# Retention attention and a sine-gated feed-forward: a re-planned table of steps, without dummy transfers and with last stores of 128 rows

## The chip, the cores and the metric

The kernel runs on one core of a Trainium2 chip. The metric is the device time of one execution in microseconds; the times of a kernel are the median of several executions, and one more execution is recorded by the profiler. The engines are PE (matrix products, with its weight loads shown as PEld), DVE, ACT and POOL (element-wise work), and SP, which here only issues transfers (DMAs).

## The reference

Two parts follow each other. The first is a causal attention without softmax for 8 batches, 8 heads, 576 positions and 64 numbers per head; its scores are damped by the distance. Its result is read as 4608 tokens of 512 numbers and goes through a feed-forward with a sine.

```python
scores = scale * np.matmul(q, k.transpose(0, 1, 3, 2))
rel = pos[:, None] - pos[None, :]
Dmat = np.where(rel >= 0, gamma[:, None, None] ** rel[None, :, :], 0.0)
x = np.matmul(scores * Dmat, v)          # read as (4608, 512)
h = x @ w_in                             # 512 x 2048
s = np.sin(alpha * h)
g = h + s * s / (alpha + 1e-09)
out = g @ w_out                          # 2048 x 512
```

## The kernel before

**Blocks.** The first 512 tokens of each batch form blocks 0 to 7. The last 64 tokens of all batches together form block 8, the "ends". A block goes through attention (of its batch), the product with w_in in 16 chunks of 128 columns (`project`, four matmuls of 128 x 512 each), `sine` and `square` (mostly ACT), `product` (DVE), and the product with w_out. Blocks 0 to 2 do this last product plainly (`gemm2`, stored by `finish`); blocks 3 to 8 save one of eight quarter products by the scheme of Strassen and Winograd: `weight_sum` and `row_sum` prepare sums, `part_product 8 3` is the third of the seven products of block 8 (16 matmuls of 128 x 256 for each half), and `after_product` adds its bank to a kept part on DVE and stores the result.

**The table.** The whole order is a table of some 1200 lines, written out by hand, one step a line; a loop runs them, and each engine executes its instructions in the order in which the steps stand. Nothing reorders them. A step such as `crossed 5 0 q @qT2` names the batch 5, the half 0 of its tokens, the operand, and after the @ the buffer that its result gets. Six buffers raw0 to raw5 take all loads of 256 tokens in turn, so a load waits until the cast that reads its buffer has ended. Tags such as m0, h2 or op name banks of PSUM, where PE's products are kept until another engine has read them.

**From a load to PE.** `load 5 q 1` has SP fetch the second 256 tokens of batch 5's queries as 512 KB (L1358); keys and values of batches 4 to 7 come in four transfers of 128 KB (L1353). `cast` (L1404, L1330 for values) scales and rounds them to 16 bits, mostly on POOL. `crossed` (L1426) has SP issue a transposing transfer, which gives PE keys and queries with the head dimension on the partitions (tiles kT and qT). Batches 0 and 1 are transposed on PE (`turn`, `take`). Loads with the last number 2 fetch the last 64 tokens of a batch (L1365; tiles qs, ks, vs). `at.outer` multiplies keys and values on PE (L1514), `at.scores` queries and keys (L1572).

**SP's queue.** SP issues loads, transposes and stores one after the other; when one has to wait (for a cast, for a buffer, for the result to store), all behind it wait as well. Eight semaphores serve SP's transfers in turn, so that each also waits for the landing of the one eight issues earlier. `fill_up` (L1930) issues a dummy transfer of 16 KB that takes a place in this turn.

**The last stores.** Block 8 holds 64 tokens of each of eight batches. A tile `osb` of 128 rows holds two batches, whose rows lie 576 rows apart in the output; `store` writes each half of 64 rows with its own transfer (L1868).

Of the kernel before, what the change touches and what calls it, by code (L numbers as in the profile page):

```python
# [32 lines left out]
invert_alpha
cast 0 v 0 A @v162
# [4 lines left out]
take 0 q 0 A @qT1  # L39
# [16 lines left out]
cast 0 v 1 A @v163
load 1 q 1 @raw5
# [3 lines left out]
keep_busy 1 h1  # L61
# [25 lines left out]
take 1 q 0 V @qT0  # L87
# [16 lines left out]
sine 0 6 @s3  # L104
project 0 7 m1
sine 0 7 @s0
project 0 0 op
square 0 7 A @ss0
sine 0 0 @s2
# [3 lines left out]
load 1 k 0 @raw2  # L113
load_w_out 0
load_w_out 1
cast 1 k 0 G @k163
project 0 4 m0
sine 0 4 @s0
square 0 4 A @ss0
# [4 lines left out]
sine 0 8 @s2  # L124
square 0 8 A @ss2
# [6 lines left out]
take 1 k 0 V @kT1  # L132
sine 0 11 @s1
at.more 0 3 @s320
square 0 11 G @ss1
product 0 11
sine 0 9 @s2
square 0 9 G @ss0
product 0 9
sine 0 5 @s0  # L140
square 0 5 A @ss2
project 0 10 m0
sine 0 10 @s3
# [6 lines left out]
sine 0 14 @s0  # L150
square 0 14 A @ss0
project 0 12 h1
sine 0 12 @s0
# [4 lines left out]
sine 0 13 @s2  # L158
# [4 lines left out]
sine 0 15 @s2  # L163
load 1 v 0 @raw3
cast 1 v 0 G @v162
# [11 lines left out]
cast 1 k 1 G @k162  # L177
# [7 lines left out]
cast 1 v 1 A @v163  # L185
product 0 15
turn 1 k 1 h0
take 1 k 1 V (1) @kT1
# [13 lines left out]
load 2 q 1 @raw0  # L202
load 2 k 1 @raw1
cast 2 k 1 G @k160
# [3 lines left out]
load 2 k 0 @raw3  # L208
load 3 k 1 @raw4
cast 3 k 1 G @k162  # L210
load 2 v 0 @raw5
load 3 k 0 @raw1
wait_for_w_out 1
load 2 v 1 @raw0
# [4 lines left out]
at.keep 1 0 V @xT0  # L219
at.next_sum 1 3  # L220
crossed 2 1 k @kT0
# [3 lines left out]
crossed 2 1 q @qT1  # L225
crossed 2 0 k @kT3
crossed 2 0 q @qT2
# [14 lines left out]
project 1 6 h1  # L242
gemm2 0 3 h0
sine 1 7 @s3
sine 1 6 @s0
# [4 lines left out]
sine 1 13 @s0  # L250
project 1 8 op
sine 1 8 @s1
square 1 13 V @ss0
product 1 13
square 1 8 V @ss2
square 1 7 V @ss0
product 1 8
project 1 11 h1
sine 1 11 @s2
square 1 11 A @ss3  # L260
# [3 lines left out]
square 1 10 A @ss1  # L264
# [4 lines left out]
sine 1 5 @s1  # L269
square 1 5 A @ss3  # L270
project 1 9 h2
sine 1 9 @s0
# [7 lines left out]
cast 3 k 0 G @k163  # L280
at.more 2 1 @s321
at.more 2 2 @s321
# [7 lines left out]
square 1 9 V @ss3  # L290
product 1 9
at.masked 2 1 1 @ret0
square 1 14 A @ss1
product 1 14
sine 1 1 @s1
square 1 1 A @ss0
# [8 lines left out]
square 1 0 A @ss3  # L305
sine 1 4 @s2
square 1 4 A @ss0
sine 1 3 @s0
square 1 3 A @ss2
# [17 lines left out]
sine 1 15 @s3  # L327
# [5 lines left out]
sine 1 12 @s2  # L333
square 1 12 V @ss2
# [13 lines left out]
crossed 3 1 k @kT1  # L348
cast 4 q 1 G @q160
cast 3 q 1 G @q161  # L350
at.more 3 2 @s320
# [4 lines left out]
crossed 3 0 k @kT0  # L356
# [45 lines left out]
sine 2 0 @s3  # L402
square 2 0 A @ss1
# [28 lines left out]
square 2 13 G @ss3  # L432
# [7 lines left out]
at.more 4 1 @s321  # L440
# [26 lines left out]
sine 2 12 @s1  # L467
# [66 lines left out]
product 3 5
sine 3 4 @s3
at.masked 4 0 0 @ret0
at.scores 4 0 1 m0
cast 5 k 0 G @k162
square 3 4 A @ss2
product 3 4  # L540
at.scores 4 1 0 m1
at.masked 4 1 0 @ret1
finish 2 1
cast 5 v 1 G @v163
cast 5 q 1 G @q160
project 3 8 h2
project 3 10 h1
at.masked 4 0 1 @ret2
sine 3 6 @s2
gemm2 2 8 op  # L550
project 3 9 m0
sine 3 8 @s0
square 3 8 A @ss1
product 3 8
load 5 q 0 @raw4
sine 3 10 @s3
project 3 11 h2
square 3 10 A @ss0
gemm2 2 9 op
gemm2 2 10 op  # L560
crossed 5 0 k @kT1
load 6 v 0 @raw0
gemm2 2 11 op
square 3 6 A @ss2
product 3 6
cast 5 q 0 G @q162
sine 3 9 @s0
square 3 9 A @ss2
product 3 9
sine 3 11 @s2  # L570
square 3 11 A @ss3
finish 2 2
load 1 k 2
project 3 12 h0
at.scores 4 1 1 m1
product 3 10
at.outer 5 (0,1) op h1
at.evict_bank 5 0 A @kvs0
at.evict_bank 5 1 A
at.values 4 0 False m0 relay=G  # L580
product 3 11
project 3 13 h2
at.masked 4 1 1 @ret3
at.values 4 1 False m1 relay=G
row_sum 3 S3 0 V
load 6 k 0 @raw1
sine 3 13 @s2
weight_sum T2 0 V
at.values 4 0 True
at.add_states 4 0  # L590
at.values 4 1 True
weight_sum T3 1 V
cast 6 k 0 G @k161
row_sum 3 S2 0 V
crossed 5 0 q @qT2
sine 3 12 @s3
square 3 12 A @ss3
cast 6 v 0 G @v160
weight_sum T2 1 V
product 3 12  # L600
at.add_states 4 1
load 6 v 1 @raw4
project 3 15 h1
cast 6 v 1 G @v161
square 3 13 A @ss0
product 3 13
gemm2 2 12 op
at.keep 4 0 A @xT1
at.keep 4 1 A
gemm2 2 13 op  # L610
gemm2 2 14 op
weight_sum T1 1 V
sine 3 15 @s3
square 3 15 A @ss3
product 3 15
row_sum 3 S1 0 V
gemm2 2 15 op
finish 2 3
project 3 14 h0
at.to_state 5 0 @s161  # L620
at.scores 5 0 1 m1
at.masked 5 0 1 @ret2
sine 3 14 @s3
square 3 14 A @ss3
product 3 14
load 7 v 0 @raw4
weight_sum T4 0 V
at.more 5 1 @s320
project 4 0 h2
sine 4 0 @s2  # L630
row_sum 3 S3 1 V
part_product 3 1 op
after_product 3 1
square 4 0 A @ss2
product 4 0
weight_sum T1 0 V
project 4 2 m0
sine 4 2 @s0
square 4 2 A @ss3
product 4 2  # L640
at.more 5 2 @s320
project 4 1 h1
sine 4 1 @s3
square 4 1 A @ss1
at.scores 5 0 0 m1
product 4 1
row_sum 3 S2 1 V
crossed 5 1 q @qT3
load 6 q 0 @raw1
cast 6 q 0 G @q162  # L650
weight_sum T4 1 V
project 4 4 h0
sine 4 4 @s0
square 4 4 A @ss0
row_sum 3 S1 1 V
project 4 3 h2
sine 4 3 @s3
at.to_state 5 1
part_product 3 2 - first=1
project 4 6 m0  # L660
square 4 3 A @ss2
product 4 3
crossed 5 1 k @kT1
project 4 5 h1
after_product 3 2
sine 4 6 @s3
sine 4 5 @s1
square 4 5 A @ss2
square 4 6 A @ss3
at.masked 5 0 0 @ret0  # L670
part_product 3 6 op
load 6 q 1 @raw0
product 4 4
at.scores 5 1 0 m1
product 4 5
after_product 3 6
project 4 7 h0
sine 4 7 @s2
square 4 7 A @ss0
project 4 9 h2  # L680
row_sum 3 S4 0 V
sine 4 9 @s2
project 4 8 h1
at.to_state 5 2
product 4 7
part_product 3 7 - first=6
sine 4 8 @s1
square 4 9 A @ss0
at.masked 5 1 0 @ret1
load 6 k 1 @raw2  # L690
product 4 6
square 4 8 A @ss3
at.more 5 3 @s320
project 4 10 h0
sine 4 10 @s2
at.to_state 5 3
after_product 3 7
at.scores 5 1 1 m1
at.masked 5 1 1 @ret3
at.values 5 0 False m0 relay=G  # L700
part_product 3 5 op
square 4 10 A @ss1
at.values 5 0 True
cast 0 q 2 G
at.add_states 5 0
at.keep 5 0 A @xT0
project 4 11 m1
sine 4 11 @s1
row_sum 3 S4 1 V told_to=G
crossed 6 0 k @kT2  # L710
product 4 8
cast 0 k 2 G
after_product 3 5
part_product 3 3 - first=5
product 4 9
product 4 10
after_product 3 3
project 4 12 h2
square 4 11 A @ss1
sine 4 12 @s3  # L720
project 4 13 h0
sine 4 13 @s2
load 2 v 2
square 4 12 A @ss0
load 3 v 2
product 4 11
cast 6 k 1 G @k163
at.values 5 1 False m1 relay=G
at.outer 6 (0,1) op h1
at.evict_bank 6 0 A @kvs0  # L730
at.evict_bank 6 1 A
square 4 13 A @ss3
crossed 6 0 q @qT2
product 4 12
at.values 5 1 True
at.add_states 5 1
part_product 3 4 m0
project 4 14 h1
row_sum 4 S3 0 V
load 7 q 0 @raw1  # L740
after_product 3 4
at.keep 5 1 A
at.more 6 1 @s320
sine 4 14 @s0
square 4 14 A @ss0
cast 6 q 1 G @q162
row_sum 4 S2 0 V
fill_up
project 5 0 m1
row_sum 4 S3 1 V  # L750
sine 5 0 @s2
square 5 0 A @ss2
load 1 v 2
product 4 14
project 4 15 m0
cast 0 v 2 G
at.to_state 6 0 @s161
product 5 0
crossed 6 1 k @kT3
part_product 4 1 op  # L760
project 5 1 h2
at.scores 6 0 1 m1
project 5 3 h1
product 4 13
sine 4 15 @s2
square 4 15 A @ss0
product 4 15
after_product 4 1
part_product 4 2 - first=1
load 7 k 1 @raw0  # L770
sine 5 1 @s2
square 5 1 A @ss0
sine 5 3 @s2
load 2 q 2
square 5 3 A @ss2
project 5 2 h0
row_sum 4 S1 0 V
crossed 6 1 q @qT3
at.masked 6 0 1 @ret2
load 3 q 2  # L780
after_product 4 2
at.more 6 2 @s321
at.more 6 3 @s321
at.to_state 6 3
cast 7 v 0 G @v162
product 5 1
row_sum 4 S2 1 V
row_sum 4 S4 0 V
load 7 k 0 @raw2
cast 7 k 0 G @k161  # L790
at.to_state 6 1
sine 5 2 @s0
square 5 2 A @ss1
product 5 2
project 5 4 h2
sine 5 4 @s0
square 5 4 A @ss3
part_product 4 6 op
product 5 3
row_sum 4 S4 1 V told_to=G  # L800
project 5 5 h0
after_product 4 6
sine 5 5 @s2
product 5 4
square 5 5 A @ss2
project 5 6 h1
sine 5 6 @s0
# [437 lines left out]
def kernel(  # L1245
# [18 lines left out]
    nc = tc.nc  # L1264
# [641 lines left out]
    at = [Attention(b) for b in range(B)]  # L1906
# [136 lines left out]
```

## Time and profile before

| | |
|---|---|
| median of 3 runs | 306.46 us (306.09 to 306.5) |
| profiled execution | 307.99 us, its span 306.3 us |
| mean granted clock of PE | 0.969 |
| busy: PE, DVE, ACT, POOL | 287.7, 220.2, 220.0, 138.0 us |
| transferred | 50.08 MB, mean 164 GB/s |

The span runs from the first to the last recorded instruction or landing; the profiled execution's own time has 1.7 us around it. In a row of a timeline the first number is the start in us, the second the duration, then come the engine, the line, the operation, output and inputs, the number of like instructions joined in the row, and in brackets the idle time ahead of it with what ended it. SPq and ACTq are the issuing of transfers by those engines; a transfer lands later than its issue ends. "Granted clock" is the share of full speed at which PE ran.

### The profile page before, as it was taken

Reading aid. Unit: us, or ns where it says so; the run is one execution under the profiler, and the core shown is the slowest. Engines: PE = TensorE matmul, PEld = TensorE weight load, DVE = VectorE, ACT = ScalarE, POOL = GpSimd, SP = SyncE. Lnnn points to the kernel's source line nnn. Section 1 sums busy time; section 2 is a strip of 40 time slices with the busy share of each in tenths; the row PEclk is TensorE's granted clock in tenths of the full one; section 3 lists DMA queues with packets and bytes.
Section 4 is the critical chain, followed back from the end, with each engine's and each line's share of the span. In section 5 each row is a group of like instructions: output and inputs, shape, how many; then the busy total and the mean of one; then the engine's idle time right before and its main releaser. Section 6 shows DMA issues by size and latency. Waiting matters only on the chain. (4 is left out here: it accounts for less than half of the span.)

```text
span 306.3 us, 8404 instructions
## 1 busy us (share of the span) xinstructions
PE 287.7 (94%) x3480; PEld 183.5 (60%) x3480; DVE 220.2 (72%) x316; ACT 220.0 (72%) x361; POOL 138.0 (45%) x151
## 2 busy tenths in 40 slices
PE   5789999999989999995999999999999999999982
PEld 3556555555445544542667666776676667667871
DVE  2577988779257686694588689778976777687771
ACT  1577946996776997792786986898878978788400
POOL 4773778573878674324475374950551100000000
PEclk9589999999999999996899999999999999999998
DMA  7999999988797879968692898898315302110123
GB/s 224 337 214 212 258 296 318 221 237 241 187 229 201 135 161 207 222 156 191 137 256 56 184 203 200 159 129 201 76 54 139 96 13 71 36 43 7 61 71 102
DMA packets 123014, 50.08 MB, mean 164 GB/s; under 512 B 79968, under 2 KB 120928, under 8 KB 122976
## 3 DMA queue, kind: packets, MB, share of 16 engines
q1 hardware_dynamic: 119456, 45.17, 61.8%
q0 software_dynamic: 2688, 4.19, 7.5%
q8 instruction: 27, 0.44, 0.6%
q10 hardware_dynamic: 832, 0.18, 0.3%
q14 instruction: 11, 0.09, 0.1%
HBM read 36.75 MB, written 9.44 MB: 151 GB/s over the span
## 5 line engine op out<-in xcount | busy, mean ns | idle before, releaser
L1777 DVE SCALAR_TENSOR_TENSOR gT<-ss,inva,hps 128x512 f16<-128x512 f16 x144 | 104.0, 742 | 46.0 <-ACT ss L1770 43.3
L1753 PE MATMUL hps<-xT,w_in 128*128 128x512 f16 (+1 forms) x532 | 121.8, 374 | 0.2 <-DVE xT L1330 0.2
L1761 ACT ACTIVATE s<-hps,alpha_t 128x512 f16<-128x512 f32 x144 | 96.5, 682 | 32.1 <-PE hps L1753 30.5
L1753 PEld LDWEIGHTS <-w_in 128*128 128x128 f16 x596 | 66.0, 115 | 50.0 <-issue 1.4
L1770 ACT ACTIVATE ss<-s 128x512 f16<-128x512 f16 x125 | 77.4, 629 | 6.0 <-DVE gT L1777 3.1
L1793 PE MATMUL ops<-w_out,gT 128*128 128x512 f16 x192 | 45.6, 379 | 0.0
L1857 PEld LDWEIGHTS <-gT 128*128 128x128 f16 x384 | 38.0, 100 | 8.8 <-issue 0.6
L1404 POOL TENSOR_TENSOR k<-raw,cn 128x1024 f16<-128x1024 f32 (+1 forms) x17 | 30.5, 1794 | 20.8 <-DMA raw<-in_k_dram 20.7
L1857 PEld LDWEIGHTS <-S 128*128 128x128 f16 x288 | 27.8, 98 | 7.6 <-DVE osb L1903 1.8
L1404 POOL TENSOR_TENSOR q<-raw,cn 128x1024 f16<-128x1024 f32 x13 | 24.9, 1921 | 15.3 <-DMA raw<-in_q_dram 11.6
L1793 PEld LDWEIGHTS <-gT 128*128 128x128 f16 x192 | 18.1, 98 | 20.8
L1857 PE MATMUL hps<-w_out,gT 128*128 128x256 f16 x192 | 24.5, 285 | 0.0
L1857 PE MATMUL hps<-w_out,S 128*128 128x256 f16 x192 | 23.0, 273 | 1.6 <-DVE osb L1903 1.6
L1857 PE MATMUL hps<-T,gT 128*128 128x256 f16 x192 | 22.8, 273 | 0.0
L1584 DVE TENSOR_TENSOR ret<-sc,mask 128x1024 f16<-128x1024 f32 x16 | 19.2, 1219 | 4.1 <-PE sc L1572 4.1
L1584 DVE TENSOR_TENSOR ret<-sc,mask_halved 128x768 f16<-128x768 f32 x16 | 15.2, 952 | 6.4 <-PE sc L1572 6.3
L1559 POOL TENSOR_TENSOR s<-kvs,cn 128x256 f32<-128x256 f32 x21 | 14.0, 666 | 12.5 <-ACT kvs L1328 11.3
L1328 ACT CAST xT<-o 128x1024 f16<-128x1024 f32 (+1 forms) x15 | 16.3, 1129 | 4.0 <-PE o L1636 4.0
L1840 DVE TENSOR_TENSOR S<-gT,S 128x1024 f16<-128x1024 f16 x24 | 17.7, 743 | 0.3 <-PE hps L1857 0.2
L1560 POOL TENSOR_TENSOR kvs<-s,kvs 128x256 f32<-128x256 f32 x21 | 16.0, 760 | 4.0 <-ACT kvs L1328 1.4
L1572 PEld LDWEIGHTS <-kT 64*64 64x64 f16 x512 | 8.3, 113 | 14.7 <-issue 13.9
L1572 PE MATMUL sc<-qT,kT 64*64 64x128 f16 (+1 forms) x512 | 12.2, 225 | 5.1 <-DMA qT<-q 5.1
(78 smaller groups left out, 265.3 us busy)
## 6 DMA issues: line engine op xcount, KB each, us to landing
raw<-in_q_dram SPq DMA_DIRECT2D x16, 512.0 KB, 5.1
out_dram<-osb SPq DMA_DIRECT2D x32, 256.0 KB, 2.7
raw<-in_k_dram SPq DMA_DIRECT2D x8, 512.0 KB, 6.1
raw<-in_v_dram SPq DMA_DIRECT2D x8, 512.0 KB, 7.0
raw<-in_v_dram SPq DMA_DIRECT2D x32, 128.0 KB, 3.1
raw<-in_k_dram SPq DMA_DIRECT2D x32, 128.0 KB, 3.3
w_in<-in_moe_w_in_dram POOLq DMA_DIRECT2D x4, 512.0 KB, 12.1
w_out<-in_moe_w_out_dram POOLq DMA_DIRECT2D x4, 512.0 KB, 13.5
```

The lines of the kernel that those rows point to most:

```text
L1328: eng.copy(d_, s_)
L1404: eng.tensor_tensor(dst[:, a0:a1].rearrange("p a r t d -> p t (a r) d"), t_.rearrange("p (t a) x -> p t a x", t=2)[:, :, a0:a1].rearrange( ...
L1560: nc.gpsimd.tensor_tensor(self.kvs[:, c], s32, self.kvs[:, c], ADD)
L1572: matmul(sc[halves(g), t, c : c + n], kT[halves(t), 2 * a + r, halves(g)], qT[halves(t), 2 * a : 2 * a + 2, 64 * g + i0 : 64 * g + 64], st ...
L1584: nc.vector.tensor_tensor(ret.rearrange("p t (z x) -> p (t z) x", z=2)[:, :, 0:n], sc.rearrange("p t (z x) -> p (t z) x", z=2)[:, :, 0:n], ...
L1753: matmul(hps_of[n, fc][0][:, cols], w_in16[fc // 4][:, a, fc % 4 :: 4], xs[n][:, a, cols], start=(a == 0 and part != 1), stop=(a == KT - 1 ...
L1761: nc.scalar.activation(s_t, hps, mybir.ActivationFunctionType.Sin, bias=0.0, scale=alpha_t[:, fc : fc + 1],)
L1770: nc.scalar.activation(ss_t, s_t, mybir.ActivationFunctionType.Square)
L1777: nc.vector.scalar_tensor_tensor(gT[n][:, fc, :], ss_t, inva[:, fc : fc + 1], hps, MULT, ADD)
L1793: matmul(ops[n, c, cols.start][:, cols], gT[n][:, fk, c * P : (c + 1) * P], w_out16[:, fk, cols], start=(fk == 0), stop=(fk == FC - 1), sk ...
L1840: made = eng.tensor_tensor(out_, x, y, op)
L1857: matmul(acc[:, 256 * j : 256 * j + 256], lhs[:, x, 128 * j : 128 * j + 128], rhs[:, x], start=(tag is not None and j == js[0] and p == 0 ...
```

## The change

The table is written anew: the same steps in another order, other buffers for loads and transposes, other banks. `fill_up` and its eight steps are gone. `store` writes the 128 rows of a tile of block 8 with one transfer, and deals the two tiles of a call to the two queues named.

```diff
     def store(n, t, e, osb, js=(0, 1), issue=(nc.sync, nc.sync)):
         cols = slice(256 * e, 256 * e + 256)
         if n == 8:
-            for r in range(2):
-                for j in js:
-                    issue[r].dma_start(rows_of_ends(2 * t + j)[r, :, cols], osb[halves(r), j])
+            for j in js:
+                issue[j].dma_start(rows_of_ends(2 * t + j)[:, :, cols], osb[:, j])
             return
...
-    PAD = 8
-
-    def fill_up():
-
-        nc.sync.dma_start(gate, w_out16[:, 0, 0:64])
-
```

Of the table, a few lines (apart in the table):

```diff
-load 2 v 0 @raw5
+load 2 v 0 @raw2
...
-load 2 v 1 @raw0
+load 2 v 1 @raw3
...
-part_product 8 3 h2 (0)
-part_product 8 3 op (1)
+part_product 8 3 m1 (1)
+part_product 8 3 m0 (0)
```

In the rows below, a name's trailing number tells buffers apart within one of the two programs only; x4 joins like rows. The line numbers of the changed kernel are lower by 8 to 9 than those of the kernel before: L1418 is L1426, L1345 is L1353, L1350 is L1358, L1357 is L1365.

**SP in block 5.** Before, from the load of batch 5's first queries on (it is the row `raw_153<-in_q`):

```order
L1358 DMA raw_153<-in_q_dram 128x8x128
L1426 DMA_TRANSPOSE kT_619<-k_129 128x8x128
L1353 DMA raw_123<-in_v_dram 64x8x64 x4
L1786 DMA out_dram<-osb 128x512
L1365 DMA ks_2044<-in_k_dram 64x8x64
L1353 DMA raw_765<-in_k_dram 64x8x64 x4
L1426 DMA_TRANSPOSE qT_271<-q_141 128x8x128
```

After, from the load of its first queries (`raw_243<-in_q`) on:

```order
L1350 DMA raw_243<-in_q_dram 128x8x128
L1357 DMA qs_2031<-in_q_dram 64x8x64
L1345 DMA raw_287<-in_v_dram 64x8x64 x4
L1357 DMA qs_2098<-in_q_dram 64x8x64
L1357 DMA vs_2100<-in_v_dram 64x8x64 x2
L1418 DMA_TRANSPOSE qT_272<-q_1523 128x8x128
L1418 DMA_TRANSPOSE kT_260<-k_155 128x8x128
```

The turned queries of batch 5 (the transpose into qT) left SP behind four loads of batch 6's values and four of its keys, and now leave ahead of both. The four loads of values that stand ahead of it now are of batch 5 itself.

**SP in block 2.** Before, with the buffers' full names:

```order
L1358 DMA raw4_153<-in_k_dram 128x8x128
L1358 DMA raw5_125<-in_v_dram 128x8x128
L1358 DMA raw1_765<-in_k_dram 128x8x128
L1926 DMA gate_78<-w_out16_74 128x64
L1358 DMA raw0_123<-in_v_dram 128x8x128
L1426 DMA_TRANSPOSE kT0_964<-k160_902 128x8x128
```

After:

```order
L1350 DMA raw3_153<-in_k_dram 128x8x128
L1350 DMA raw2_125<-in_v_dram 128x8x128
L1350 DMA raw1_287<-in_k_dram 128x8x128
L1917 DMA gate_78<-w_out16_74 128x64
L1350 DMA raw3_153<-in_v_dram 128x8x128
L1418 DMA_TRANSPOSE kT3_196<-k161_155 128x8x128
```

The order is the same. The second load of values of batch 2 went to raw0, and now goes to raw3, the buffer into which batch 3's keys were loaded three loads ahead of it.

**SP at the end.** Before:

```order
L1365 DMA vs_4156<-in_v_dram 64x8x64
L1932 DMA gate<-w_out_74 128x64
L1871 DMA out_dram<-osb 128x2x256 x4
L1932 DMA gate<-w_out_74 128x64 x3
L1871 DMA out_dram<-osb 128x2x256 x3
L1868 DMA out_dram<-osb 64x256 x14
```

After:

```order
L1357 DMA vs_4184<-in_v_dram 64x8x64 x2
L1418 DMA_TRANSPOSE qTs<-qs_4182 128x4x128
L1418 DMA_TRANSPOSE qTs<-qs_4153 128x4x128
L1862 DMA out_dram<-osb 128x2x256 x7
L1859 DMA out_dram<-osb 2x64x256 x7
```

Fourteen stores of 64 x 256 became seven of 2 x 64 x 256 (the shape is that of the addresses in the output), and the dummies on w_out between the earlier stores are gone. Of the last two halves of block 8, ACT issues the two of 64 rows before, and one of 128 rows after.

More of the change, by code (lines that the diff above doesn't have):

```diff
@@ L600 @@
[L600 to L606, printed above, removed]
+at.add_states 4 1
+load 2 v 2
+load 3 v 2
+project 3 13 h2
+load 6 v 0 @raw4
+project 3 12 h0
+weight_sum T2 1 V
+at.scores 5 0 1 m0
+at.masked 5 0 1 @ret3
+sine 3 13 @s1
+crossed 5 1 q @qT3
 gemm2 2 12 op
[L608 removed]
+square 3 13 A @ss1
+sine 3 12 @s1
+weight_sum T1 0 V
+square 3 12 A @ss0
 at.keep 4 1 A
+cast 6 v 0 G @v161
+at.more 5 1 @s320
 gemm2 2 13 op
 gemm2 2 14 op
[L612 removed]
+product 3 13
@@ L701 @@
[L701 to L712, printed above, removed]
+project 4 3 m1
+sine 4 3 @s3
+square 4 3 A @ss2
+load 6 q 1 @raw4
+row_sum 3 S2 1 V
+row_sum 3 S1 1 V
+cast 6 q 1 G @q160
+at.to_state 5 1
+project 4 4 h0
+project 4 6 h2
+sine 4 4 @s3
+product 4 2
+product 4 3
+load 0 k 2
+weight_sum T1 1 V
+product 4 1
+load 6 k 0 @raw2
+load 1 k 2
@@ new lines @@
+part_product 3 2 - first=1
+after_product 3 2
+at.scores 5 1 0 m1
+sine 4 6 @s0
+at.masked 5 1 0 @ret0
+load 7 k 1 @raw4
+square 4 4 A @ss0
+product 4 4
+project 4 7 m0
+part_product 3 6 op
+after_product 3 6
+at.scores 5 0 0 m1
+square 4 6 A @ss2
+product 4 6
+project 4 5 h1
+at.masked 5 0 0 @ret2
+sine 4 5 @s2
+at.more 5 3 @s321
+at.to_state 5 3
+square 4 5 A @ss3
+product 4 5
+project 4 9 h0
+sine 4 9 @s3
+load 6 v 1 @raw0
+square 4 9 A @ss0
+sine 4 7 @s1
+part_product 3 7 - first=6
+project 4 12 h2
@@ L713 @@
+sine 4 12 @s3
+product 4 9
+after_product 3 7
+cast 6 q 0 G @q162
+at.values 5 0 False m1 relay=G
+crossed 2 2 q
+square 4 12 A @ss1
+project 4 10 h0
+row_sum 3 S4 1 V told_to=G
+part_product 3 5 op
+square 4 7 A @ss0
+product 4 7
+at.values 5 0 True
+at.add_states 5 0
+load 7 v 1 @raw1
+at.to_state 5 2
+project 4 8 h1
+cast 6 v 1 G @v162
+sine 4 10 @s1
+crossed 6 0 q @qT2
+cast 6 k 0 G @k161
+project 4 11 m0
+at.keep 5 0 A @xT0
+row_sum 3 S4 0 V
+at.scores 5 1 1 m1
+cast 2 v 2 G
 after_product 3 5
@@ L714 @@
 part_product 3 3 - first=5
-product 4 9
-product 4 10
[L717 to L729, printed above, removed]
+crossed 6 0 k @kT2
+product 4 12
+at.masked 5 1 1 @ret2
+sine 4 8 @s2
+square 4 8 A @ss2
+product 4 8
+sine 4 11 @s0
+square 4 11 A @ss1
+project 4 13 h2
+at.values 5 1 False m1 relay=G
+square 4 10 A @ss2
+crossed 6 1 k @kT3
@@ new lines @@
+after_product 4 1
+sine 5 3 @s0
+cast 7 v 1 G @v160
+project 5 2 h0
+sine 5 2 @s3
+cast 0 k 2 G
+at.masked 6 0 1 @ret2
+square 5 3 A @ss2
+product 5 1
+product 5 3
+square 5 2 A @ss3
+load 7 q 0 @raw0
+part_product 4 2 - first=1
+at.more 6 3 @s321
+after_product 4 2
+project 5 5 m0
+load 7 k 0 @raw1
+cast 7 k 0 G @k161
+product 5 2
+row_sum 4 S2 1 V
+project 5 7 h2
+row_sum 4 S1 1 V
+sine 5 5 @s1
+square 5 5 A @ss2
+row_sum 4 S4 1 V told_to=G
+project 5 4 h1
+project 5 6 h0
+product 5 5
+sine 5 4 @s3
@@ new lines @@
+square 5 4 A @ss1
+load 4 v 2
+load 5 v 2
+at.scores 6 1 0 m1
+at.masked 6 1 0 @ret1
+at.to_state 6 1
+part_product 4 6 op
+after_product 4 6
+cast 2 k 2 G
+sine 5 6 @s1
+square 5 6 A @ss3
+product 5 4
+product 5 6
+cast 7 k 1 G @k163
+cast 7 q 0 G @q160
+project 5 10 m0
+load 4 k 2
+sine 5 7 @s3
+square 5 7 A @ss2
+at.scores 6 1 1 m1
+part_product 4 7 - first=6
+at.masked 6 1 1 @ret3
+sine 5 10 @s2
+square 5 10 A @ss3
+project 5 9 h1
+sine 5 9 @s0
+product 5 7
+after_product 4 7
+project 5 8 h0
@@ new lines @@
+row_sum 6 S3 0 V
+cast 7 q 1 G @q162
+crossed 7 1 q @qT3
+product 6 8
+product 6 4
+sine 6 7 @s0
+at.more 7 3 @s321
+project 6 11 h2
+square 6 7 A @ss3
+load 5 k 2
+sine 6 9 @s0
+square 6 9 A @ss0
+after_product 5 7
+cast 4 v 2 G
+crossed 7 1 k @kT3
+at.values 7 0 False m0 relay=G
+at.scores 7 1 0 m1
+product 6 7
+product 6 9
+sine 6 11 @s2
+part_product 5 5 op
+at.values 7 0 True
+at.add_states 7 0
+square 6 11 A @ss1
+at.keep 7 0 A @xT0
+at.masked 7 1 0 @ret2
+at.scores 7 1 1 m1
+product 6 11
@@ new lines @@
+project 6 10 h1
+project 6 13 h2
+project 6 12 h0
+sine 6 10 @s1
+square 6 10 A @ss1
+sine 6 12 @s2
+square 6 12 A @ss3
+at.masked 7 1 1 @ret0
+at.values 7 1 False m1 relay=G
+row_sum 5 S4 0 V
+after_product 5 5
+at.to_state 7 1
+row_sum 5 S4 1 V told_to=G
+product 6 10
+project 6 14 m0
+product 6 12
+sine 6 14 @s0
+sine 6 13 @s1
+at.values 7 1 True
+at.add_states 7 1
+at.keep 7 1 A
+load 6 q 2
+load 7 k 2
+row_sum 6 S2 0 V
+square 6 14 A @ss3
+product 6 14
+crossed 2 2 k
+part_product 5 3 - first=5
@@ L1082 @@
-product 7 7
+cast 4 q 2 G
+part_product 6 2 - first=1
+after_product 6 2
+square 7 3 A @ss1
+product 7 1
+project 7 2 h1
+load 7 q 2
+cast 6 q 2 G
+load 6 v 2
+ends.scores 0 m1
+ends.masked 0
+sine 7 2 @s1
+project 7 7 h2
+square 7 2 A @ss3
+project 7 8 h0
+product 7 2
+product 7 3
+load 7 v 2
+project 7 5 m0
+project 7 4 m1
+sine 7 8 @s3
+square 7 8 A @ss3
+row_sum 6 S1 0 V
+product 7 8
+sine 7 7 @s0
+square 7 7 A @ss1
+product 7 7
+sine 7 4 @s0
+project 7 6 h1
+row_sum 7 S3 0 V
+part_product 6 6 op
@@ L1083 @@
+project 7 9 h0
+sine 7 5 @s1
+square 7 5 A @ss3
+row_sum 6 S1 1 V
+crossed 6 2 q
+after_product 6 6
+project 7 13 h2
+square 7 4 A @ss1
+cast 6 v 2 G
+product 7 4
+product 7 5
+part_product 6 7 - first=6
+after_product 6 7
+ends.values 0 False m0
+crossed 4 2 q
+sine 7 6 @s0
+ends.scores 2 m1
+ends.masked 2
+square 7 6 A @ss2
+at.to_state 7 3
+ends.values 0 True
 ends.add_states 0
 ends.keep 0 0 A
-fill_up
+ends.keep 0 1 A
+sine 7 9 @s3
+sine 7 13 @s0
+square 7 13 A @ss1
+square 7 9 A @ss0
+part_product 6 5 op
```

1221 lines of the change are left out of this document (495 added, 726 removed).

## The prediction

> **What bounds the kernel now.** I read the page's clock and span first, then the engines' busy shares, the waits of PE, a table of windows, and last the timelines of the places where PE stands.
>
> ```profile
> span 306.3 us, 8404 instructions
> PE 287.7 (94%) x3480; PEld 183.5 (60%) x3480; DVE 220.2 (72%) x316; ACT 220.0 (72%) x361; POOL 138.0 (45%) x151
> PE sc L1572 <- DMA qT<-q: 5.1, 2, 4.0
> PE hps L1857 <- DVE osb L1903: 1.6, 1, 1.6
> ...
> 130.00:140.00 10.00, 7.61 (x132) 3.86 (x118) 8.58 (x11) 8.72 (x13) 2.26 (x2) 1.00 0.71 169
> 140.00:150.00 10.00, 8.44 (x63) 4.70 (x64) 4.28 (x7) 3.27 (x6) 7.22 (x8) 0.66 0.60 144
> 150.00:160.00 10.00, 10.00 (x80) 6.63 (x79) 8.11 (x13) 8.39 (x15) 5.01 (x6) 1.00 1.06 240
> ```
>
> The second and third row give a wait as total, times, longest; in the windows PE's busy time comes first and the granted clock stands ahead of the last two numbers. PE is the bound: busy in 94% of the span. No other engine passes 72%. So time can only be won where PE stands, at a lowered clock, or behind its last matmul. Two waits on a transposed query sum to 5.1 us, one on an output buffer's addition is 1.6. The longest, 4.0, lies in the windows around 140, and the window after it ran at 0.66 of the clock.
>
> ```profile
> 136.59 1.03 PE L1753 MATMUL hps<-xT,w_in 128*128 128x512 f16 x4
> 141.56 0.54 PE L1572 MATMUL sc<-qT,kT 64*64 64x128 f16 x16 [3.95 <-DMA qT<-q]
> 142.03 1.90 PE L1753 MATMUL hps<-xT,w_in 128*128 128x512 f16 x4
> 130.85 2.11 POOL L1404 TENSOR_TENSOR q<-raw,cn 128x1024 f16<-128x1024 f32 x1 [0.70 <-DMA raw<-in_q_dram]
> 130.18 3.76 SPq L1353 DMA_DIRECT2D raw<-in_v_dram  x4
> 134.04 0.57 SPq L1786 DMA_DIRECT2D out_dram<-osb  x1
> 134.65 0.61 SPq L1365 DMA_DIRECT2D ks<-in_k_dram  x1
> 135.31 2.70 SPq L1353 DMA_DIRECT2D raw<-in_k_dram  x4
> 138.11 1.30 SPq L1426 DMA_TRANSPOSE qT<-q  x1
> ```
>
> This is the stall. Batch 5's second query cast (the later of the two, so the safe one) ended on POOL at 130.85+2.11 = 132.96. Its transpose left SP only at 138.11, because SP first issued four value loads, a store, a key load and four loads of batch 6's keys. PE idled 3.95 us, and the four matmuls that take 1.03 us at 136.59 took 1.90 at 142.03. The clock of 0.66 over ten us costs (1 - 0.66) x 10 = 3.4 us. Stall and slow clock together: 7.35 us. [...]
>
> **Step 1, turned queries ahead (block 5).** In the new order crossed 5 0 q stands ahead of the four loads of batch 6's values and keys: only three small tail loads remain between the last loads of batch 5 and it. The transposes depend on casts that ended by 133 before, so the whole 7.35 goes: -7.35. What is late next is the cast of batch 5's second half of values, on POOL behind both query casts and the first value cast, while the values' matmuls need it; with the loads issued in the new order I place its end about 0.5 us behind PE's arrival. I take +1.0, between 0 and 3.4 (a wait long enough to slow the clock once more costs about as much again as before).
>
> **Step 2, loads of blocks 2 and 3.** Here the buffers rotate otherwise.
>
> ```profile
> 47.17 1.38 SPq L1358 DMA_DIRECT2D raw<-in_v_dram  x1
> 51.63 1.47 SPq L1358 DMA_DIRECT2D raw<-in_v_dram  x1
> 53.16 2.80 SPq L1426 DMA_TRANSPOSE kT<-k  x1
> 50.28 1.90 POOL L1404 TENSOR_TENSOR q<-raw,cn 128x1024 f16<-128x1024 f32 x1
> 52.14 2.88 POOL L1404 TENSOR_TENSOR k<-raw,cn 128x1024 f16<-128x1024 f32 x1
> 57.67 2.02 POOL L1330 CAST v<-raw 128x1024 f16<-128x1024 f32 x2 [2.65 <-DMA raw<-in_v_dram]
> 60.92 0.71 PE L1514 MATMUL kv<-v,k 64*64 64x64 f16 x64
> 90.84 0.64 PE L1572 MATMUL sc<-qT,kT 64*64 64x128 f16 x32 [1.17 <-DMA qT<-q]
> ```
>
> The second value load of batch 2 is put into the buffer that holds batch 3's keys, so it waits until their cast ends: 52.14+2.88 = 55.02 instead of 51.63, 3.4 us later. Everything behind it on SP, four transposes and the next loads, goes back with it. The value casts that ended at 59.69 would end near 62, behind PE's arrival at 60.92. Part of the lag reaches the wait at 90.84, whose transpose is queued on SP behind the same line. Gains in the start-up (a query load without a wait and a free bank for the first turn) are absorbed at the same place. I take +2.5, between 0 and 3.4.
>
> **Step 3, the tail of the computation.**
>
> ```profile
> 295.83 1.91 PE L1857 MATMUL hps<-w_out,S 128*128 128x256 f16 x16
> 299.30 1.92 PE L1857 MATMUL hps<-w_out,S 128*128 128x256 f16 x16 [1.56 <-DVE osb L1903]
> 293.81 0.68 DVE L1903 TENSOR_TENSOR osb<-hps,low 128x512 f32<-128x512 f32 x1
> 301.26 0.42 DVE L1903 TENSOR_TENSOR osb<-hps,mid 128x256 f32<-128x256 f32 x1 [0.45 <-PE hps L1857]
> 294.52 9.27 SPq L1868 DMA_DIRECT2D out_dram<-osb  x14
> 300.85 1.38 ACTq L1868 DMA_DIRECT2D out_dram<-osb  x2
> ```
>
> The last product no longer uses the bank that the product before it is being read from, so PE's wait of 1.56 goes. SP issues 7 stores in place of 14: 9.27/14 = 0.66 each, so its last store need not leave at 303.1 but when its data is ready. By this alone the end would come about 2.6 us earlier (1.56 of the bank, 1.4 of the queue, less 0.42 for the exchanged order of the halves on DVE). This counts only if the stores then still land quickly.
>
> **Step 4, the stores of 128 rows.** This is the operation the trace doesn't show. The old stores are 64 rows of 1 KB. The new one takes the last 64 tokens of two batches, which lie apart in the output, so its list of addresses is 2 x 64 x 256, with the two slabs outermost; 8 of them move the 1 MB that 16 moved.
>
> ```profile
> q1 hardware_dynamic: 1392, 1.18, 21.8%
> out_dram<-osb SPq DMA_DIRECT2D x14, 64.0 KB, 2.0
> out_dram<-osb SPq DMA_DIRECT2D x1, 256.0 KB, 2.5
> GB/s 0 0 0 28 155 155 326 338 246 337 346 345 349 348 345 347 346 346 348 348 345 347 346 346 348 348 327 331 312 327 234 197 204 210 224 209 217 219 214 211
> ```
>
> The first three rows are of the stretch from 290 us on; the last is GB/s in 40 slices of the first 20 us. 14 stores of 64 packets of 1 KB and one of 256 are 1152; 1392 - 1152 = 240 = 15 x 16. So each of these stores ends with 16 small packets, one for each DMA engine: it was cut into 16 equal shares. All of them have 64 or 128 rows as their outermost count. The two bounds follow: if the new store is also cut in 16, it costs nothing and step 3 gives -2.6. If the shares are cut along the outermost count, two slabs give two shares, and 14 engines stand idle. Then each of the two engines moves 64 packets for a store and 8 x 64 = 512 in all. A packet costs (2.5 - 2.0) us / 12 = 42 ns by the two landing times (16 against 4 packets an engine), or 16 x 1 KB / 346 GB/s = 47 ns by the busiest stretch. 512 x 42 ns = 21.5 us. The first store is issued at 294.52, when its addition on DVE ends, and its data starts about 1.5 us later, at 296. So the last lands at 317.5, where it was 303.1 + 2.0 = 305.1: +12.4, and step 3's gain is no longer on the path, since the engines' queue starts with the first store. I take this bound, 0.6 against 0.4: the nearest rows in size land in 2 us, but none starts with a count under 64, while the sixteen equal shares of every row fit a cut along that count, and this change is the first to make it 2.
>
> [...]
>
> **Step 5, dummy transfers.**
> ```profile
> 243.75 0.64 SPq L1932 DMA_DIRECT2D gate<-w_out  x1
> 229.25 0.42 PE L1675 MATMUL scs<-qTs,kTs 64*64 64x64 f16 x32
> 60.00:90.00 30.00, 29.57 (x397) 15.21 (x395) 19.11 (x28) 25.05 (x45) 19.75 (x22) 1.00 0.91 226
> 90.00:110.00 20.00, 19.07 (x289) 10.54 (x290) 14.68 (x20) 14.73 (x29) 15.49 (x18) 1.00 0.79 167
> ```
>
> Eight dummies leave SP's queue, about 0.64 us each there, between stores that nothing on PE waits for: 0. Loads of the tails that come later serve matmuls that begin at 229: 0. The transposes of the other blocks stay some 1.5 to 2 us ahead of their users when I lay the new order over the old durations: 0, with the chance of a wait of 1 us. The two windows are for the second rival.
>
> **Sum.** 306.3 - 7.35 + 1.0 + 2.5 + 12.4 = 314.85 us of span. The profiled execution took 307.99 us with its span of 306.3, but the median of the runs, 306.46, lies only 0.16 above the span; so the forecast for the median is 315.0.
>
> **Rivals.**
> 1. The new store is cut in sixteen, like all others: 306.3 - 7.35 + 1.0 + 2.5 - 2.6 = 299.85, median 300.0, faster. For it: every store of the profile is cut so and lands in 2.0 to 2.7 us. Against it: none of these begins with a 2. Its place is the last ten us, and the number of engines decides: without the tail the sum is 302.45, so the tail may cost 3.85 before the gain is gone. With four shares the data takes 10.7 us and ends at 306.7, 1.6 behind before: still faster. With two it isn't.
> 2. The order gives back what the stall gave: the wait for the value cast in block 5 grows to 3.4 us and slows the clock again, +6.4 in place of +1.0, with the stores in sixteen shares: 306.3 - 7.35 + 6.4 + 2.5 - 2.6 = 305.25, median 305.4; with blocks 2 and 3 at their upper bound 306.3, no change. For it: POOL waited for a load ahead of its casts there before too (0.70 at 130.85). Against it: the wait of 1.17 at 90.84 left the clock at 1.00 in the windows on both sides, so a short one costs no more than itself.
> 3. Two shares, and a dearer packet: at 47 ns 24.1 us and the sum 317.6; at 50 ns (21.8% of 16 engines in 20 us, over 1392 packets) 25.6 and 319.1.
>
> **How the numbers follow.** Two shares at any of the prices: 0.60, with its own range of 310.5 (all of step 1's and 2's costs at nothing, 42 ns, and 1 us less) to 319. Sixteen shares with a wait of one us or so: 0.32, range 298.5 to 303. Rival 2, and a cut into some number between: 0.08, half of it within 0.2%. A difference under 0.2% (0.6 us) is about what a measurement of this kernel can't tell from none. Slower 0.62, same 0.03, faster 0.35. The cases of both signs carry weight, so the range for 8 in 10 runs from 299.3, which leaves out the lower part of rival 1, to 318.5.
>
> **What would show it.** Step 1: no wait on qT near 130 to 142, and a clock of 1.00 in each ten us from 30 to 290. Step 2: a second value load of batch 2 that leaves SP near 55, a wait of PE on v at about 61, and one over 2 us near 89. Step 3: the last 32 matmuls without a wait in them. Step 4 right: the new stores' times to landing grow from 3 us with the first to over 15 with the last, GB/s in the last stretch near 45, and small packets two a store; wrong: landing in about 2.2 us each, and an end some 4 us after PE's last matmul. The forecast fails as a whole if the stores land fast, since they carry more than all other steps together.

## The result, and the profile after

The changed kernel takes 323.27 us (322.95 to 323.46), against 306.48 for the kernel before on the same chip: 1.0522 times as long, 95% interval 1.045 to 1.0594. The forecast said slower, 315.0, with 318.5 as its upper end. The direction held, the size did not.

The page of the changed kernel first: span, busy shares, then the windows (PE's busy time first, the granted clock ahead of the last two numbers) and PE's waits (total, times, longest).

```profile
span 321.5 us, 8399 instructions
PE 287.3 (89%) x3480; PEld 183.2 (57%) x3480; DVE 223.6 (70%) x316; ACT 219.4 (68%) x361; POOL 138.7 (43%) x151
...
10.00:20.00 10.00, 8.67 (x220) 5.96 (x219) 8.69 (x15) 6.89 (x13) 6.92 (x8) 1.00 1.15 247
20.00:30.00 10.00, 3.47 (x25) 2.71 (x22) 1.62 (x3) 0.73 (x1) 3.74 (x4) 0.67 1.15 215
130.00:140.00 10.00, 10.00 (x220) 5.45 (x218) 8.69 (x12) 8.77 (x14) 5.46 (x5) 1.00 0.85 168
140.00:150.00 10.00, 10.00 (x56) 5.77 (x55) 8.05 (x12) 9.53 (x16) 3.38 (x4) 1.00 0.92 229
300.00:321.00 21.00, 0.73 (x7) 0.40 (x5) 1.06 (x3) 0.00 (x0) 0.00 (x0) 0.58 0.13 45
...
PE tr L1428 <- POOL q L1396: 6.5, 1, 6.5
PE sc L1564 <- DMA qT<-q: 0.5, 1, 0.5
```

The old stall is gone: from 130 to 150 PE is busy all the time at full clock. Two things are new. First, near 20 PE waits 6.5 us once, and the clock is 0.67 in that window. Before, the windows from 10 and from 20 looked like this, with the lowered clock ahead of 20 and no such wait:

```profile
10.00:20.00 10.00, 8.68 (x160) 5.68 (x163) 6.84 (x9) 5.94 (x11) 9.69 (x11) 0.61 1.16 276
20.00:30.00 10.00, 9.01 (x125) 6.40 (x118) 7.54 (x16) 7.29 (x13) 3.32 (x4) 1.00 1.19 213
```

Second, from 300 on hardly any engine works while 45 GB/s flow. The end, in the timeline and in the transfers from 285 on:

```profile
297.07 3.66 PE L1849 MATMUL hps<-w_out,S 128*128 128x256 f16 x32
300.77 0.76 DVE L1894 TENSOR_TENSOR osb<-hps,mid 128x256 f32<-128x256 f32 x2 [0.46 <-PE hps L1849]
295.77 16.72 SPq L1859 DMA_DIRECT2D out_dram<-osb  x7
301.55 1.12 ACTq L1859 DMA_DIRECT2D out_dram<-osb  x1
...
GB/s 0 195 68 0 0 249 13 254 25 0 0 0 33 33 42 48 48 49 48 48 48 25 48 49 48 48 48 48 48 48 48 49 47 49 46 1 0 0 0 0
DMA packets 1857, 1.85 MB, mean 46 GB/s; under 512 B 64, under 2 KB 1856, under 8 KB 1856
```

The last 32 matmuls run without a wait, so the bank's wait is gone too. DVE is done at 301.5, yet the last data lands at 320.06 (before, 304.88). The stores flow at 48 GB/s, where the plain stores ahead of them reach 250. As in the prediction, I read the small packets as one for each engine at the end of a store, and so they count the engines: 64 = 3 x 16 + 8 x 2, three plain stores with sixteen each and eight new ones with two each.

### The profile page after: what moved, and what is told of

Read it like the earlier page. It is cut to its first block, busy times and chain, and to the rows that moved or that the text cites. A ratio compares the mean times of both kernels' runs of the same rounds, so it can differ in the third digit from the quotient of the medians.

```text
span 321.5 us, 8399 instructions
## 1 busy us (share of the span) xinstructions
PE 287.3 (89%) x3480; PEld 183.2 (57%) x3480; DVE 223.6 (70%) x316; ACT 219.4 (68%) x361; POOL 138.7 (43%) x151
## 4 chain that ended last, share of the span: by engine, by line
PE 67%; DMA 12%; POOL 6%; SPq 6%; issue 1%; DVE 1%; ACT 0%; DVEq 0%; POOLq 0%; ACTq 0%
PE hps L1745 32%; PE hps L1849 20%; PE ops L1785 8%; DMA raw<-in_q_dram 7%; POOL q L1396 4%; SPq L1345 3%; DMA qT<-q 3%; PE sc L1564 2%; DMA raw<-in_v_dram 2%; PE o L1606 2%; SPq L1350 1%; POOL k L1396 1%; PE kv L1506 1%; SPq L1418 1%; POOL kvs L1552 1%
## 5 line engine op out<-in xcount | busy, mean ns | idle before, releaser
L1849 PEld LDWEIGHTS <-gT 128*128 128x128 f16 x384 | 37.4, 98 | 8.2 <-issue 0.3
L1785 PEld LDWEIGHTS <-gT 128*128 128x128 f16 x192 | 18.0, 98 | 20.7 <-DVE gT L1769 0.2
L1849 PE MATMUL hps<-w_out,gT 128*128 128x256 f16 x192 | 22.8, 273 | 0.0
L1832 DVE TENSOR_TENSOR S<-gT,S 128x1024 f16<-128x1024 f16 x24 | 21.7, 909 | 0.8 <-PE hps L1849 0.6
L1544 POOL TENSOR_TENSOR s<-kvs,cn 128x256 f16<-128x256 f32 x17 | 11.6, 683 | 20.6 <-PE o L1606 14.6
L1322 POOL CAST v<-raw 128x1024 f16<-128x1024 f32 x10 | 10.3, 1039 | 19.9 <-DMA raw<-in_v_dram 17.6
L1551 POOL TENSOR_TENSOR s<-kvs,cn 128x256 f32<-128x256 f32 x21 | 13.3, 634 | 9.9 <-ACT kvs L1320 7.3
```

The lines of the kernel that those rows point to most:

```text
L1551: nc.gpsimd.tensor_tensor(s32, self.kvs[:, c - 1], g1.unsqueeze(2).to_broadcast([P, 4, D]), MULT)
L1785: matmul(ops[n, c, cols.start][:, cols], gT[n][:, fk, c * P : (c + 1) * P], w_out16[:, fk, cols], start=(fk == 0), stop=(fk == FC - 1), sk ...
L1832: made = eng.tensor_tensor(out_, x, y, op)
L1849: matmul(acc[:, 256 * j : 256 * j + 256], lhs[:, x, 128 * j : 128 * j + 128], rhs[:, x], start=(tag is not None and j == js[0] and p == 0 ...
```

## The experiments

"Before" is the kernel before on the chip of the same run; its median there was 306.8 to 307.75.

**The old stores in the changed kernel.**

```diff
-            for j in js:
-                issue[j].dma_start(rows_of_ends(2 * t + j)[:, :, cols], osb[:, j])
+            for r in range(2):
+                for j in js:
+                    issue[r].dma_start(rows_of_ends(2 * t + j)[r, :, cols], osb[halves(r), j])
```

> The changed kernel with the stores of 64 rows put back in block 8, all else as changed. Theory (a store of 2 x 64 rows runs on two DMA engines only): PE ends as in the changed kernel near 300.7, SP issues 14 stores at 0.64 us, ten of them from 298.7 on, so the last lands near 306.5 and the median is 307.5 to 308.5, 15 us under the changed kernel. Rival (the tail is long because SP holds the queue, whatever the shape): the end stays above 315.

309.11 us, 1.0046 (1.0006 to 1.0087) of before, about 1 us more than I expected; the changed kernel stood at 1.0522. The difference of the ratios, 0.0476, is 14.6 us. The rival's end above 315 did not come.

**The new stores in the kernel before** (the same edit the other way).

> The kernel before with only the stores of block 8 changed to 128 rows. Theory: the first is issued at 294.5 as before, eight stores of 64 packets on each of two engines at 42 to 43 ns take 22 us, the last lands near 318.4; median 319 to 321. Rival (only the new order makes the stores late): not above 308.

320.61 us, 1.0391 (1.0265 to 1.0516), 13.0 us more than before. Its issue row and its packets from 290 on:

```profile
295.74 15.76 SPq L1867 DMA_DIRECT2D out_dram<-osb  x7
DMA packets 1585, 1.59 MB, mean 45 GB/s; under 512 B 48, under 2 KB 1584, under 8 KB 1584
```

48 = 2 x 16 + 8 x 2, and 15.76 us for seven issues: the long end belongs to the shape of the store and needs nothing of the new order.

**An earlier load at the start of the changed kernel.**

```diff
-load 1 q 0 @raw0
+load 1 q 0 @raw2
```

> The changed kernel with one buffer changed: the load of batch 1's first queries goes to raw2 instead of raw0, so it needn't wait for the cast of batch 0's second queries. Theory (the load that left SP 1 us later fell behind POOL's weight loads and landed some 7 us later): the load leaves at 9.4, lands by 16, PE's wait of 6.5 us near 20 goes and the median falls by 5 to 6.5, to 317 to 318.5. Rival (the load is slow because all loads of the start share the engines, whenever it is issued): it lands after 20 still, and under 2 us are won.

315.66 us, 1.0252 (1.017 to 1.0334). The profiled span fell from 321.5 to 313.9, by 7.6, more than expected. The load now leaves even earlier than in the kernel before, and PE gets to its first products at 20.94 (before 22.67, changed 27.38). The row of the start of each, SP's two query loads and POOL's cast of the second; first before, then changed, then this run:

```profile
8.05 3.90 SPq L1358 DMA_DIRECT2D raw<-in_q_dram  x2
11.50 2.43 POOL L1318 DMA_DIRECT2D w_in<-in_moe_w_in_dram  x3
17.27 1.92 POOL L1404 TENSOR_TENSOR q<-raw,cn 128x1024 f16<-128x1024 f32 x1
31.67 0.61 PE L1436 MATMUL tr<-ident,k 128*128 128x128 f16 x8
```

```profile
7.96 5.05 SPq L1350 DMA_DIRECT2D raw<-in_q_dram  x2
11.47 2.43 POOL L1310 DMA_DIRECT2D w_in<-in_moe_w_in_dram  x3
24.60 1.89 POOL L1396 TENSOR_TENSOR q<-raw,cn 128x1024 f16<-128x1024 f32 x1 [7.40 <-DMA raw<-in_q_dram]
26.55 1.03 PE L1428 MATMUL tr<-ident,q 128*128 128x128 f16 x8 [6.53 <-POOL q L1396]
37.43 0.61 PE L1428 MATMUL tr<-ident,k 128*128 128x128 f16 x8
```

```profile
7.85 2.94 SPq L1350 DMA_DIRECT2D raw<-in_q_dram  x2
17.09 1.92 POOL L1396 TENSOR_TENSOR q<-raw,cn 128x1024 f16<-128x1024 f32 x1
```

The end of the issue row is what matters: 11.95 before, 13.01 in the changed kernel, 10.79 here. Between before and the changed kernel, a load issued one microsecond later has its cast 7.3 us later. In this time, from 11.5 on, POOL issues three loads of weights.

**Both edits in the changed kernel.**

> Both edits of the two runs above: stores of 64 rows and the query load to raw2. If the two costs are independent they add: 307.5 to 308.5 less 5 to 6.5, so 301.5 to 303.5, some 1.3% below the kernel before. Rival (the time won at the start is lost again at later waits): within 1 us of the run with old stores alone.

301.80 us, 0.9804 (0.9721 to 0.9889); 7.3 us under the run with old stores alone. The two costs add up, and without them the change is a gain of 5.8 us.

**The late load in the kernel before.**

```diff
-load 1 q 0 @raw4
+load 1 q 0 @raw0
```

> The kernel before with one buffer changed: the load of batch 1's first queries goes to raw0 (free when DVE's cast of batch 0's second queries ends, 12.6) instead of raw4 (11.5). Theory (leaving SP 1 us later puts it behind POOL's three weight loads of 11.5): it lands near 24 instead of 16.9, PE waits 4 to 6 us there, median 310.5 to 313. Rival (it needs something else of the new order to be slow): under 1.5 us.

313.21 us, 1.0186 (1.0106 to 1.0266), 6.4 us more.

```profile
24.41 1.89 POOL L1404 TENSOR_TENSOR q<-raw,cn 128x1024 f16<-128x1024 f32 x1 [7.07 <-DMA raw<-in_q_dram]
26.35 1.03 PE L1436 MATMUL tr<-ident,q 128*128 128x128 f16 x8 [4.58 <-POOL q L1404]
```

One name of a buffer brings the late cast into the old order; PE waits 4.58 us there instead of 6.53, since it gets there later.

**The weight loads later in the changed kernel.**

```diff
-load_w_in 1
-load_w_in 2
 at.to_state 0 0 A @s161
...
 at.to_state 0 1 G
+load_w_in 1
+load_w_in 2
```

> The changed kernel with the second and third weight loads on POOL moved behind its cast of batch 1's second queries (issued near 17 instead of 12 to 14); the query load keeps its buffer and still leaves SP at 12.6. Theory (it is these loads that hold the engines): it lands near 18 to 19, PE's wait of 6.5 us falls under 2, and the median falls by 3 to 6 unless the weights then come late. Rival (a load that leaves at 12.6 lands after 22 whatever POOL does): no change.

317.18 us, 1.028 (1.0209 to 1.0352): 6.4 us less over before than the changed kernel (10.35 against 16.8).

```profile
8.13 5.04 SPq L1350 DMA_DIRECT2D raw<-in_q_dram  x2
19.39 1.90 POOL L1396 TENSOR_TENSOR q<-raw,cn 128x1024 f16<-128x1024 f32 x1 [0.49 <-DMA raw<-in_q_dram]
21.86 0.93 PE L1428 MATMUL tr<-ident,q 128*128 128x128 f16 x8
```

The query load leaves as late as in the changed kernel, but is cast at 19.39 instead of 24.60. So it was slow because two more loads of weights were issued around the time that it left.

**No dummies in the kernel before** (the eight lines `fill_up` taken out).

> The kernel before without its eight dummy transfers. Theory: nothing, within 0.6 us of before. Rival (they set the turn of the semaphores, so that stores or loads wait for other landings): over 1 us either way.

307.04 us, 1.0001 (0.9963 to 1.0039). Within this interval, about 1.2 us either way, they cost nothing and bring nothing.

**One transpose ahead in the kernel before.**

```diff
 cast 5 q 0 G @q162
+crossed 5 0 q @qT2
...
-crossed 5 0 q @qT2
```

> The kernel before with one line moved: the transpose of batch 5's first queries stands right behind their cast, ahead of the loads of batch 6's keys. Theory: the wait of 3.95 us at 141 and the slow clock behind it go, median 299 to 301. Rival (SP waits for the cast with the loads behind it, and a later wait takes the place): 303 or more.

309.37 us, 1.0067 (1.0028 to 1.0106): about 2 us slower, not 6 faster. The rival was right. The transpose of the second keys, before and then in this run, and what waits for it here:

```profile
150.63 1.30 SPq L1426 DMA_TRANSPOSE kT<-k  x1
150.86 1.30 SPq L1426 DMA_TRANSPOSE kT<-k  x1
156.31 0.53 PE L1572 MATMUL sc<-qT,kT 64*64 64x128 f16 x16 [6.92 <-DMA kT<-k]
150.00:160.00 10.00, 3.69 (x24) 1.52 (x25) 2.73 (x5) 1.84 (x4) 5.30 (x7) 0.60 1.10 254
```

The wait at 141 is gone, and PE comes to the next scores of the block earlier, but their keys leave SP at 150.86, behind loads of batch 6 and no earlier than before. A wait of 6.92 and a clock of 0.60 take it all back.

**Three transposes ahead.** In addition (the second keys now go to the buffer kT3; with kT0 in its place the steps would wait for each other in a circle):

```diff
+crossed 5 1 k @kT3
...
 at.add_states 4 1
+crossed 5 1 q @qT3
...
-crossed 5 1 q @qT3
...
-crossed 5 1 k @kT1
```

> The kernel before with three transposes of batch 5 ahead of batch 6's loads: the first queries behind their cast, the second keys right behind them (into kT3), the second queries behind the last use of their buffer. Theory (moving one transpose only hands the wait to the next one behind the loads; the gain needs all of them ahead): neither the wait at 141 nor that at 156 is left, median 299 to 301. Rival (SP then issues batch 6's loads later, and block 6 waits for them instead): 304 or more.

306.78 us, 0.9972 (0.9939 to 1.0006): no gain that is clear of zero, and at most 1.9 us. The wait has moved from SP to POOL.

```profile
155.87 2.35 POOL L1404 TENSOR_TENSOR q<-raw,cn 128x1024 f16<-128x1024 f32 x1 [4.13 <-DMA raw<-in_q_dram]
160.84 0.37 PE L1614 MATMUL o<-ret,v 64*64 64x128 f16 x16 [3.97 <-POOLq L1468]
```

POOL waits for the load of batch 6's queries ahead of a cast, and a mark that lets PE go on with batch 5's values is queued behind it.

**The three transposes and that cast.**

```diff
-cast 6 q 0 G @q162
...
 at.values 5 0 True
+cast 6 q 0 G @q162
```

> The run before (three transposes of batch 5 ahead) with one more line moved: POOL casts batch 6's first queries behind the relay between the two halves of batch 5's values instead of ahead of it. Theory (in the run before POOL waited 4.1 us for the load of these queries, and PE waited 4.0 us for the relay queued behind that cast): the wait at 160.8 and its slow clock go, and the whole 7 us of the first wait is won: median 299.5 to 302. Rival (the loads of batch 6 are late by then, and the wait moves on to another step of block 6): 304.5 or more.

301.77 us, 0.9808 (0.9748 to 0.9868), 5.85 us less than before. Now the long waits of this block are gone:

```profile
150.00:160.00 10.00, 9.08 (x108) 5.95 (x108) 9.02 (x12) 6.70 (x10) 8.78 (x11) 1.00 0.91 236
```

**The first two stores alone as two slabs** (in the kernel with early load and 64-row stores).

```diff
+            if (t, e) == (0, 0):
+                for j in js:
+                    issue[j].dma_start(rows_of_ends(2 * t + j)[:, :, cols], osb[:, j])
+                return
```

> The changed kernel with the early query load and 64-row stores, but the first two of block 8's stores (its second product) written as 2 x 64 rows. Theory (two engines are busy 2 x 64 x 46 ns = 5.9 us from 290.8 on and free again when the last stores come): within 1.5 us of the run with all stores of 64 rows, 300.5 to 303. Rival (each such store costs its eighth of the 15 us, wherever it stands): 304.5 to 306.

302.70 us, 0.984 (0.9764 to 0.9916), against 0.9804 with 64-row stores throughout: intervals that overlap. Two stores on two engines with other work behind them cost 0.9 us by the medians (301.80 without), which these intervals can't tell from nothing; eight in a row at the end cost 13 to 15 us.

**The best version: 128 KB a store with 64 outermost** (in the same kernel with early load and 64-row stores; the last two tiles still go out in stores of 64 KB).

```diff
+            ends_of = out.rearrange("(c r s) d -> r s c d", r=2, s=S)
             for r in range(2):
-                for j in js:
-                    issue[r].dma_start(rows_of_ends(2 * t + j)[r, :, cols], osb[halves(r), j])
+                c0 = 2 * t + js[0]
+                issue[r].dma_start(ends_of[r, 512:576, c0 : c0 + len(js), cols], osb[halves(r), js[0] : js[-1] + 1])
```

> The changed kernel with the early query load, and block 8's stores cut the other way: one of 64 rows x 2 tiles x 256 numbers (128 KB, 64 outermost) for each half of the partitions. Theory (64 outermost gives sixteen shares, and half the issues): SP needs 8 stores in place of 14, the last leaves when its data is ready near 295.2, 2 to 3 us are won against the 64-row stores; median 298.5 to 300.5. Rival (128 KB with two rows apart is slow whatever stands outermost): above 310.

299.05 us, 0.973 (0.9666 to 0.9793), 8.2 us under before and the fastest of all.

```profile
288.00 7.10 SPq L1861 DMA_DIRECT2D out_dram<-osb  x8
out_dram<-osb SPq DMA_DIRECT2D x6, 128.0 KB, 2.4
```

The same 128 KB as in the new store, also in 1 KB pieces from distant rows, land in 2.4 us. What the slow store has that this one hasn't is a count of 2 outermost. Its 128 partitions aren't the cause: the plain stores of 256 KB have them as well and reach 250 GB/s.

## Why the prediction was right and wrong

Between the two profiled spans lie 321.5 - 306.3 = 15.2 us. I follow PE's lag at four places with equal work behind them (the parts are rounded to a tenth). At the turn of batch 1's keys it is 37.43 - 31.67 = +5.8. Just ahead of the old stall it is about +6.7 (136.6 us before against 143.2 to 143.4, by the widths of the matmuls done). At the second pair of scores of block 5, with 1821 matmuls behind it in both, it is 156.08 - 156.55 = -0.5. The first store of block 8 leaves SP at 295.77 instead of 294.52: +1.25.

```profile
156.55 0.37 PE L1572 MATMUL sc<-qT,kT 64*64 64x128 f16 x16
156.08 0.37 PE L1564 MATMUL sc<-qT,kT 64*64 64x128 f16 x16
```

| part | forecast | measured |
|---|---|---|
| start | 0 ("absorbed") | +5.8 |
| blocks 1 to 4, and cast in block 5 | +3.5 | +0.9 |
| stall and slow clock in block 5 | -7.35 | -7.2 |
| blocks 5 to 8, small steps | 0 | +1.7 |
| from the first store to the last landing | +12.4 | +13.9 |
| span | +8.55 | +15.2 |
| from span to median | +0.16 | +1.77 |

**The step that failed is step 2**, with its sentence that the gains in the start-up "are absorbed". I saw a query load that no longer had to wait (batch 0's) and counted a gain; the next one, batch 1's first queries, I did not price, though its buffer had changed as well. It had to wait for DVE's cast (ended at 12.61) instead of POOL's, which ends 1 us earlier (at 11.56 before), and that microsecond put it behind the weight loads (issued from 11.47 to 13.90). Of the 8.3 us by which the forecast of 315.0 fell short, this is the largest term. Both directions are shown: the load set free in the changed kernel gives back 7 to 8 us, the same buffer put into the old kernel costs 6.4. Of the weight loads as the obstacle, moving two of them is the proof. The gains were there, too: PE reached the turn of these queries at 26.55 - 6.53 = 20.02, before at 22.21. The wait of 6.5 and the slow clock behind it (0.67 from 20 to 30) took more than that. Part of the 5.8 belongs to this execution alone: with the old stores and the same start, the late cast began at 24.28 instead of 24.60, and PE waited 5.9 for it instead of 6.5.

The rest of step 2 was right in its mechanism and too dear. Batch 2's second value load left 60.81 - 51.63 = 9.2 us later, which is the lag of 5.8 and just the 3.4 forecast. But PE waited only 0.68 for the values and 0.50 for a transposed query, and the old wait of 1.17 at 90.84 is gone from its place, now 96.65, where the lag is 5.8 again. So the 2.5 was too much by about all of it, and this hid part of the miss.

```profile
60.81 0.37 SPq L1350 DMA_DIRECT2D raw<-in_v_dram  x1
67.44 0.70 PE L1506 MATMUL kv<-v,k 64*64 64x64 f16 x64 [0.68 <-POOL v L1322]
71.63 0.42 PE L1564 MATMUL sc<-qT,kT 64*64 64x128 f16 x16 [0.50 <-DMA qT<-q]
96.65 0.64 PE L1564 MATMUL sc<-qT,kT 64*64 64x128 f16 x32
```

**Step 4 was right in kind**, and its size was 1.5 us short: 24.3 us from the first issue at 295.77 to the last data at 320.06, where I had 23.0 (with data from 297.07 on, a little sooner after the issue than the 1.5 us I took); the end before was 304.88 instead of 305.1. The price of a packet held: at the steady 48 to 49 GB/s of the row above, two engines move 1 KB each in 42 to 43 ns, so rival 3's dearer packet did not come. The 1.3 us above 23.0 lie where that row is below its steady rate: 33, 33 and 42 in the first three us of the stores, and 25 in one us near 306. Why the flow was slower there stays open. That the shares follow the outermost count is what these traces show: two small packets for each store of 2 x 64 x 256, sixteen for each of 64 x 256 (272 = 17 x 16 from 290 on with the old stores in the changed kernel), and with 64 outermost again sixteen (192 = 12 x 16 from 280 on in the best version) and a landing after 2.4 us. Other counts were not run. Rival 1 (sixteen shares) fell. Without the slow stores and the slow start, the kernel came out at 301.8 with stores of 64 rows and at 299.05 with stores of 128 KB that start with 64; rival 1's forecast was 300.0.

**Step 1 was right for the changed kernel, and wrong in its reason.** The stall went, worth 7.2 where I had 7.35, and no wait on the value cast took its place (PE 10.00 of 10 us in both windows). But I put the gain on one transpose moved ahead of batch 6's loads. That move alone made the old kernel about 2 us slower; with three moved there was no clear gain; only with POOL's order changed as well did 5.85 come. So in the old order it takes transposes and casts together. Which lines of the new table earn its 7.2 was not run. The "what is late next" that I looked for on POOL was the right question, put to the new order only. The 3.4 us that I gave step 1 and rival 2 as a wait that slows the clock was near what two waits show: in the stall the clock was 1.00 until 140.7, 3.1 us into the wait, and 0.51 from there to 147.6; in the changed kernel's wait near 20 it was 1.00 until 23.4, 3.4 us in, and 0.50 from there to 30.2.

**Step 3**: the bank's wait went, as said, and was worth nothing behind the slow stores. **Step 5** was right about the dummies: 0 to within the interval. The 1.7 us between 156 and 296 lie in steps of at most about half a microsecond that I didn't trace further; the price of 0 there was too kind.

**The offset.** Each profiled execution here takes 1.7 us more than its span. I took only 0.16, since the profiled run of before was 1.5 slower than the median of its kernel. The changed kernel's profiled run, 323.2, lay at its median. So a forecast against this span had to add back up to 1.6 us; that alone is a third of the 4.8 by which the range was missed.

## What to carry to other kernels

When a store is merged, look at the outermost count of its addresses in the output: here an outer 2 put 1 MB on two DMA engines and cost 13 to 15 us, and turning the order of the same dimensions gave it back (299.05 us against 315.66 with the same early load), with 8 issues of SP where the old stores needed 14. When the buffers rotate anew, price every load by what its buffer now waits for and by what other queues issue in the microsecond it loses, first at the start, where all loads meet. A stall that a late transpose shows need not be that transpose's alone: here moving it handed the wait to the next step of the same chain, and the gain came only when the last of them was moved.

## What the runs showed of the hardware that I had not expected

A transfer issued 1.06 us later (13.01 against 11.95, the ends of the issue rows) had its cast start 7.3 us later (24.60 against 17.27), while three weight loads were issued from another queue, from 11.5 on; with two of these moved away, a load issued as late was cast at 19.39. And SP itself is held by a store on two engines: seven issues took 16.72 us and a single one up to 5.4, where fourteen smaller ones took 9.27 before and none of them more than 0.62.
